# Attention weights divided by their row sum in front of the transposes, with scores and e in a tile per head

## The chip, the cores and the metric

The kernel runs on one core of one Trainium2 chip. The metric is the device time of one execution in microseconds (us); shorter is better. The kernel before takes 1104.95 us (median of three runs, 1103.55 to 1105.52).

## The reference

Thresholded attention with 4 batches, 8 heads, 576 positions and 64 channels per head, and behind it two feed-forward blocks on 2304 tokens:

```python
scale = 1.0 / np.sqrt(q.shape[-1])
scores = scale * np.matmul(q, k.transpose(0, 1, 3, 2))
thresh = np.max(scores, axis=-1, keepdims=True) - tau
scores = np.where(scores >= thresh, scores, -1000000000.0)
scores = scores - np.max(scores, axis=-1, keepdims=True)
attn = np.exp(scores)
attn = attn / (np.sum(attn, axis=-1, keepdims=True) + 1e-09)
x = np.matmul(attn, v)          # then x[tokens, heads * 64]
h = ((x @ w1) * (x @ w2)) @ w3 @ w_out
g = h @ w_in;  out = np.maximum(0.01 * g, g) @ w_out2
```

All inputs and the output are float32. Only the lines from `scores` to `x` are touched by the change.

## The kernel before

**Staging.** The program has two large stages. Up to about 640 us it runs the attention, and between the attention's instructions TensorE gets pieces of other work, called fillers: first the folding of w3 with w_out into one matrix (`fold_weights`, tiles ps34), then, for each batch and each of two groups of queries, the first feed-forward block (`gated`, tiles psab and psh). From about 700 us on it runs the second feed-forward block. Weights arrive as raw words and are decoded on ScalarE, VectorE and GpSimd (`stream`, L142 to L153), mostly in the first 130 us.

**Units and steps.** Heads are taken in pairs. The 576 queries of a pair are two groups: 256 queries (two chunks of 128) and 320 queries (two chunks of 128 and one of 64). A unit is one pair and one group, 32 units in all. A step is one chunk. In the 64 steps with a full chunk both heads are computed one beside the other. The 64-query chunk has one step for both heads (`c is None`): its two 64-row halves are laid over the 128 partitions through the tile qz, so it counts as one head. There are 16 such steps, 80 steps in all.

**One step.** `scores` computes the scores of a chunk of queries against all 576 keys into the PSUM tile sc (one bank per half of the keys and head), takes the negated maximum nm of each row (VectorE, L225), the threshold th (L226), and e = exp(score - max) (ScalarE, L227). `mask` sets e to zero below the threshold and adds up each row as it goes (VectorE, L241). `transposes` turns e by matmuls against an identity matrix into tp and tq, and copies these into HH and tl, with keys on the partitions. Once a unit's steps are done, `weighted` multiplies with v into the PSUM tile av, 128 channels of two heads by the unit's queries.

**The division.** It stands behind all this. av holds queries along the columns, while the row sums lie along the partitions. So `reciprocals` spreads 1 / sum on GpSimd over a tile rb, and `normalise`, a step after `weighted`, turns rb by matmuls (L322, L324) into the PSUM tile bc, multiplies xs, ScalarE's copy of av, with it on VectorE (L325), casts the product on ScalarE (L327) and has GpSimd subtract the cast from it (L328). Cast and rest are x, the input of `gated`.

**Buffers.** The pool ps_w has two PSUM buffers named w. They are shared by the fillers' sums (ps34, psab, psh), av and bc. The pool ps_a has one buffer each for sc, tp and tq. e has two buffers of two heads each.

**Order.** TensorE's instructions stand in the order in which the code is written; so do SP's until the loop has started the second `gated`. For the other engines a scheduler orders the instructions; each engine then runs its own in order. The loop of step n writes for TensorE: scores(n + 1), `weighted` of the unit that has ended, filler, first head's transposes of n, filler, second head's transposes, `normalise`, filler. So scores(n + 1) stand one step ahead of the transposes of n, and wait until mask(n) has read sc.

Of the kernel before, what the change touches and what calls it, by code (L numbers as in the profile page):

```python
# [8 lines left out]
F32 = mybir.dt.float32  # L9
# [30 lines left out]
def attention_gated_ffn(ctx: ExitStack, tc: tile.TileContext, qkv, tau, w3t, wout, w12, w2, out):  # L40
# [27 lines left out]
    pairs = cpool.tile([P, D], F32, name="pairs")
    nc.vector.tensor_tensor(out=pairs, in0=ident[:, :D], in1=ident[:, D:], op=ALU.add)
    sides = cpool.tile([P, P], F32, name="sides")  # L70
    nc.vector.memset(sides, 0.0)
    nc.vector.memset(sides[:D, :D], 1.0)
    nc.vector.memset(sides[D:, D:], 1.0)
# [4 lines left out]
    one = cpool.tile([P, 1], F32, name="one")  # L78
    nc.vector.memset(one, 1.0)
    tauc = cpool.tile([P, 1], F32, name="tauc")  # L80
    neg = cpool.tile([P, 1], F32, name="neg")
    scl = cpool.tile([P, 1], F32, name="scl")
# [116 lines left out]
            nc.vector.tensor_scalar(out=q, in0=q, scalar1=scl, scalar2=None, op0=ALU.mult))  # L199


    sc_t, e_t, stat = {}, {}, {}

    def scores(n):

        pair, g, c = STEPS[n]
        u = units.index((pair, g))
        qk = qk_t[u]
        heads = range(1 if c is None else 2)
        sc = ps_a.tile([P, 2, 2, 512], F32, tag="sc", name="sc")  # L210
        for half in range(2):
            ks = slice(half * HS, half * HS + HS)
            for a in heads:
                if c is None:
                    nc.tensor.matmul(sc[:, a, half, :HS], qz[u % 2], qk[:, ks], start=True, stop=True)
                else:
                    r = slice(a * D, a * D + D)
                    o = S + Q0[c] - GROUPS[g][0]
                    nc.tensor.matmul(sc[:, a, half, :HS], qk[r, o:o + P], qk[r, ks], start=True, stop=True)  # L219
        e = apool.tile([P, 2, S], F32, tag="e", name="e", bufs=2)  # L220
        ths = []
        for a in heads:
            nm = apool.tile([P, 1], F32, tag="nm", name="nm", bufs=4)
            th = apool.tile([P, 1], F32, tag="th", name="th", bufs=4)
            nc.vector.tensor_reduce(out=nm, in_=sc[:, a, :, :HS], op=ALU.max, axis=AX.XY, negate=True)  # L225
            nc.vector.tensor_scalar(out=th, in0=nm, scalar1=-1.0, scalar2=cb, op0=ALU.mult, op1=ALU.add)  # L226
            nc.scalar.activation(  # L227
                e[:, a].rearrange("p (a b) -> p a b", a=2), sc[:, a, :, :HS], AF.Exp, bias=nm)
            ths.append(th)
        sc_t[n], e_t[n] = (sc, ths), e  # L230

    def mask(n):
        pair, g, c = STEPS[n]
        sc, ths = sc_t.pop(n)
        key = (pair, g)
        if key not in stat:
            stat[key] = apool.tile([P, 5], F32, tag="stat", name="stat", bufs=4)
        for a, th in enumerate(ths):
            ev = e_t[n][:, a].rearrange("p (a b) -> p a b", a=2)
            o = 4 if c is None else 2 * (c % 2) + a  # L240
            nc.vector.scalar_tensor_tensor(  # L241
                out=ev, in0=sc[:, a, :, :HS], scalar=th, in1=ev, op0=ALU.is_ge, op1=ALU.mult,
                accum_out=stat[key][:, o:o + 1])

    he_t = {}

    def transposes(n):

        pair, g, c = STEPS[n]
        if (pair, g) not in he_t:
            he_t[pair, g] = apool.tile([P, 4, 2, 320], F32, tag="HH", name="HH")
        HH, tail = he_t[pair, g], tl[pair % 2]
        e = e_t.pop(n)
        tq = ps_a.tile([P, 2, P], F32, tag="tq", name="tq")
        if c is None:
            tp = ps_a.tile([P, 4, P], F32, tag="tp", name="tp")
            for kc in range(4):  # L260
                nc.tensor.transpose(tp[:, kc], e[:, 0, kc * P:kc * P + P], ident)
            nc.tensor.transpose(tq[:, 0], e[:, 0, S - P:], ident)
            nc.scalar.copy(HH[:, :, :, :D], tp.rearrange("p k (a w) -> p k a w", a=2))
            nc.vector.tensor_copy(
                tail[D:, :, :D], tq[D:, 0].rearrange("p (a w) -> p a w", a=2))
            yield
            return
        o = Q0[c] - GROUPS[g][0]
        for a in range(2):
            tp = ps_a.tile([P, 4, P], F32, tag="tp", name="tp")  # L270
            for kc in range(4):
                nc.tensor.transpose(tp[:, kc], e[:, a, kc * P:kc * P + P], ident)  # L272
# [4 lines left out]
            nc.tensor.transpose(tq[:, a], e[:, a, S - P:], ident)  # L277
            if a:
                nc.scalar.copy(tail[D:, :, o:o + P], tq[D:])
            yield  # L280

    xs_t, x_t, rb_t = {}, {}, {}

    def weighted(pair, g):

        gw = GROUPS[g][1]
        vv = vv_t[units.index((pair, g))]
        HH, tail = he_t.pop((pair, g)), tl[pair % 2]
        av = ps_w.tile([P, 512], F32, tag="w", name="av")
        for i in range(NK):  # L290
            for a in (1, 0):
                kc = (4, 0, 1, 2, 3)[i]
                rhs = (HH[:, kc, a] if kc < 4 else tail[:, a])[:, :gw]
                nc.tensor.matmul(  # L294
                    av[a * D:a * D + D, :gw], vv[:, a, kc], rhs, start=(i == 0), stop=(i == NK - 1))
        xs = apool.tile([P, 320], F32, tag="xs", name="xs", bufs=2)
        nc.scalar.copy(xs[:, :gw], av[:, :gw])
        xs_t[pair, g] = xs

    def reciprocals(pair, g):  # L300

        st = stat.pop((pair, g))
        n = 4 + g
        rr = apool.tile([P, 5], F32, tag="rr", name="rr", bufs=2)
        nc.vector.tensor_scalar(out=rr[:, :n], in0=st[:, :n], scalar1=1e-9, scalar2=None, op0=ALU.add)
        nc.vector.reciprocal(rr[:, :n], rr[:, :n])
        rb = apool.tile([P, 3, P], F32, tag="rb", name="rb")
        nc.gpsimd.tensor_tensor(
            out=rb[:, :2].rearrange("p c (h d) -> p (c h) d", h=2),
            in0=rr[:, :4].unsqueeze(2).to_broadcast([P, 4, D]),  # L310
            in1=one.unsqueeze(2).to_broadcast([P, 4, D]), op=ALU.mult)
        if g:
            nc.gpsimd.tensor_tensor(
                out=rb[:, 2], in0=rr[:, 4:5].to_broadcast([P, P]), in1=sides, op=ALU.mult)
        rb_t[pair, g] = rb

    def normalise(pair, g):
        gq, gw, cs = GROUPS[g]
        xs, rb = xs_t.pop((pair, g)), rb_t.pop((pair, g))
        bc = ps_w.tile([P, 512], F32, tag="w", name="bc")  # L320
        if g:
            nc.tensor.matmul(bc[:, :D], rb[:, 2], pairs, start=True, stop=True)  # L322
        for i, c in enumerate(cs):
            nc.tensor.transpose(bc[:, Q0[c] - gq:Q0[c] - gq + P], rb[:, i], ident)  # L324
        nc.vector.tensor_tensor(out=xs[:, :gw], in0=xs[:, :gw], in1=bc[:, :gw], op=ALU.mult)  # L325
# [130 lines left out]
    keep_busy(9)  # L456
    scores(0)
    keep_busy(10)
    weigh, norm = [], []
    filler = iter(())  # L460
    queue = []
    rate, due = 0.0, 0.0
    for n in range(NS):
# [27 lines left out]
        fill(1)  # L491
        for _ in pieces:
            pass
        if norm:
            normalise(*norm.pop())
        if last_of_unit:
            reciprocals(pair, g)
            weigh.append((pair, g))
        elif u and STEPS[n - 1][:2] != (pair, g):
            norm.append(units[u - 1])  # L500
        fill(2)
        if n < 3:
            keep_busy(7)
# [165 lines left out]
```

## Time and profile before

| | |
|---|---|
| median of three runs | 1104.95 us |
| the profiled execution | 1104.54 us |
| its span | 1102.7 us |
| TensorE matmuls busy | 1065.0 us, 97% |
| VectorE busy | 508.8 us, 46% |
| ScalarE busy | 474.0 us, 43% |
| GpSimd busy | 256.8 us, 23% |
| chain that ended last: share of TensorE | 81% |

The profile names the engines PE (TensorE's matmuls), PEld (its weight loads, which run beside the matmuls), DVE (VectorE), ACT (ScalarE), POOL (GpSimd) and SP. Times are from the start of the span. A row names the line, the engine, the operation, the tile written and the tiles read; `[1.75 <-DVE e L241]` says that the engine was idle for 1.75 us before and what it waited for. PEclk is the granted share of TensorE's clock. Matmuls overlap and their ends are modelled, so distances between starts say more than their lengths.

### The profile page before, as it was taken

To read this page: it belongs to the slowest core of one execution; us is meant where nothing else is said; L and a number is where in the kernel's file an instruction comes from. 1 tells how busy PE (TensorE), PEld (TensorE's weight loads), DVE (VectorE), ACT (ScalarE), POOL (GpSimd) and SP (SyncE) were. 2 spreads that over 40 slices of the span, in tenths; PEclk is the share of its full clock that TensorE was granted. 3 is DMA by queue.
4 is the path that set the end of the run, shared out by engine and by line. 5 is a ranking of instruction groups with operands and counts; after the bars stand their busy time and mean duration, and the time that the engine had idled before them with its cause. 6 is when DMAs were issued, how large, how long until landed. Compare 5 with 4: busy or idle time off the path is not lost.

```text
span 1102.7 us, 16185 instructions
## 1 busy us (share of the span) xinstructions
PE 1065.0 (97%) x6368; PEld 864.2 (78%) x6368; DVE 508.8 (46%) x1087; ACT 474.0 (43%) x891; POOL 256.8 (23%) x256
## 2 busy tenths in 40 slices
PE   7999799999998999999999999999999999999998
PEld 5555487789877888877898789877888888888887
DVE  5767766554666555664556633365311211111111
ACT  4767744343444444443444443477422222222232
POOL 2536712021211120120212146477400100000000
PEclk7999899999999999998999999999999999999999
DMA  9654610312112212111120023356200110010010
GB/s 305 199 198 130 204 54 23 81 35 65 40 40 63 59 30 65 44 54 51 38 62 25 1 79 114 102 191 201 72 13 1 34 34 1 5 44 1 1 39 20
DMA packets 35099, 77.59 MB, mean 70 GB/s; under 512 B 4560, under 2 KB 19408, under 8 KB 32976
## 3 DMA queue, kind: packets, MB, share of 16 engines
q1 hardware_dynamic: 34880, 76.56, 22.0%
q8 instruction: 50, 0.82, 0.3%
q14 instruction: 25, 0.20, 0.1%
q10 hardware_dynamic: 144, 0.00, 0.0%
HBM read 67.11 MB, written 9.44 MB: 69 GB/s over the span
## 4 chain that ended last, share of the span: by engine, by line
PE 81%; DVE 7%; ACT 6%; DMA 2%; issue 2%; POOL 1%; ACTq 0%; SPq 0%; DVEq 0%; POOLq 0%
PE psab L383 16%; PE po L606 16%; PE ps L584 16%; PE psh L402 9%; PE av L294 7%; PE sc L219 7%; PE tp L272 4%; PE ps L361 4%; DVE e L241 2%; ACT e L227 1%; DVE t L145 1%; ACT t L142 1%; PE tq L277 1%; ACT lw L144 1%; ACT HH L276 1%
## 5 line engine op out<-in xcount | busy, mean ns | idle before, releaser
L383 PE MATMUL psab<-x,w 128*128 128x256 f32 (+1 forms) x1536 | 234.5, 303 | 2.9 <-DVE xs L325 2.0
L383 PEld LDWEIGHTS psab<-x,w 128*128 128x128 f32 x1536 | 208.9, 189 | 24.9 <-issue 15.9
L584 PE MATMUL ps<-h,w 128*128 128x512 f32 (+1 forms) x960 | 215.7, 370 | 0.4 <-POOL w L153 0.3
L606 PE MATMUL po<-w,gg 128*128 128x512 f32 x864 | 213.8, 392 | 1.8 <-ACT gg L591 1.8
L584 PEld LDWEIGHTS ps<-h,w 128*128 128x128 f32 x960 | 169.0, 188 | 36.3 <-POOL w L153 1.3
L606 PEld LDWEIGHTS po<-w,gg 128*128 128x128 f32 x864 | 159.2, 188 | 38.1 <-ACT gg L591 3.3
L592 DVE TENSOR_TENSOR gg<-gf,gg 128x512 fp32r<-128x512 f32 (+1 forms) x80 | 61.2, 765 | 270.0 <-ACT gg L591 268.4
L225 DVE TENSOR_REDUCE nm<-sc 128x1 f32<-128x576 f32 x144 | 108.8, 756 | 108.3 <-PE sc L219 66.7
L227 ACT ACTIVATE e<-sc,nm 128x576 f32<-128x576 f32 x144 | 107.0, 743 | 117.3 <-DVE nm L225 117.0
L589 ACT ACTIVATE gf<-ps 128x512 f32<-128x512 f32 (+1 forms) x80 | 44.2, 554 | 227.0 <-PE ps L584 227.0
L241 DVE SCALAR_TENSOR_TENSOR e<-sc,th,e 128x576 f32<-128x576 f32 x144 | 112.7, 815 | 46.5 <-ACT e L227 46.5
L402 PE MATMUL psh<-gt,w 128*128 128x256 f32 (+1 forms) x768 | 115.1, 301 | 0.6 <-ACT ht L409 0.5
L394 POOL TENSOR_TENSOR gt<-at,gt 128x256 fp32r<-128x256 f32 (+1 forms) x64 | 52.7, 824 | 264.3 <-ACT gt L393 264.3
L402 PEld LDWEIGHTS psh<-gt,w 128*128 128x128 f32 x768 | 104.1, 189 | 7.7 <-issue 5.4
L219 PE MATMUL sc<-qk 64*128 64x288 f32 x512 | 81.7, 438 | 15.1 <-DVE e L241 11.2
L272 PE MATMUL tp<-ident,e 128*128 128x128 f32 x512 | 79.1, 278 | 6.0 <-ACT HH L276 6.0
L272 PEld LDWEIGHTS tp<-ident,e 128*128 128x128 f32 x512 | 61.9, 143 | 16.2 <-ACT HH L276 8.5
L151 POOL TENSOR_TENSOR lw<-t,lw 128x512 int32<-128x512 int32 x48 | 66.0, 1380 | 25.6 <-ACT lw L144 15.2
L219 PEld LDWEIGHTS sc<-qk 64*128 64x128 f32 x512 | 44.9, 188 | 33.9 <-issue 9.5
L294 PE MATMUL av<-HH,vv 128*64 128x256 f32 (+1 forms) x512 | 69.8, 416 | 0.0
L561 POOL TENSOR_TENSOR h<-hr,h 128x1024 fp32r<-128x1024 f32 (+1 forms) x10 | 23.8, 2380 | 188.2 <-DVE h L560 188.2
L361 PE MATMUL ps<-wo,w 128*128 128x512 f32 x128 | 60.0, 614 | 5.3 <-DVE xs L325 4.7
(72 smaller groups left out, 989.0 us busy)
## 6 DMA issues: line engine op xcount, KB each, us to landing
st<-in_w SPq DMA_DIRECT2D x40, 512.0 KB, 4.6
vv<-in_qkv SPq DMA_DIRECT2D x64, 160.0 KB, 2.4
raw<-in_w3t SPq DMA_DIRECT2D x8, 1024.0 KB, 5.8
qk<-in_qkv SPq DMA_DIRECT2D x32, 208.0 KB, 3.5
qk<-in_qkv SPq DMA_DIRECT2D x32, 144.0 KB, 3.0
out<-os SPq DMA_DIRECT2D x18, 256.0 KB, 2.1
raw<-in_wout SPq DMA_DIRECT2D x4, 1024.0 KB, 11.3
raw<-in_w SPq DMA_DIRECT2D x4, 1024.0 KB, 6.2
```

The costliest lines, as they stand in the source:

```text
L151: nc.gpsimd.tensor_tensor(out=lw, in0=t, in1=lw, op=ALU.add)
L219: nc.tensor.matmul(sc[:, a, half, :HS], qk[r, o:o + P], qk[r, ks], start=True, stop=True)
L225: nc.vector.tensor_reduce(out=nm, in_=sc[:, a, :, :HS], op=ALU.max, axis=AX.XY, negate=True)
L227: nc.scalar.activation(e[:, a].rearrange("p (a b) -> p a b", a=2), sc[:, a, :, :HS], AF.Exp, bias=nm)
L241: nc.vector.scalar_tensor_tensor(out=ev, in0=sc[:, a, :, :HS], scalar=th, in1=ev, op0=ALU.is_ge, op1=ALU.mult, accum_out=stat[key][:, o:o ...
L272: nc.tensor.transpose(tp[:, kc], e[:, a, kc * P:kc * P + P], ident)
L294: nc.tensor.matmul(av[a * D:a * D + D, :gw], vv[:, a, kc], rhs, start=(i == 0), stop=(i == NK - 1))
L361: nc.tensor.matmul(ps, w3_t[i][:, j * P:j * P + P], wo_t[j // 2][:, (j % 2) * 512:(j % 2) * 512 + 512], start=(j == 0), stop=(j == KF - 1))
L383: nc.tensor.matmul(ps[:, :gw], w12_t[i][:, a, mat * 512 + kk * P:mat * 512 + kk * P + P], xt[kk][:, c, :gw], start=(m == 0), stop=(m == 11))
L402: nc.tensor.matmul(ps[:, :gw], w34_t[i // 2][:, a, i % 2, o * P:o * P + P], gt[i][:, c, :gw], start=(m == 0), stop=(m == 23))
L584: nc.tensor.matmul(ps[:, :tw], w2_t[j][:, a, kk * P:kk * P + P], h3_t[ci][:, c, kk, :tw], start=(m == 0), stop=(m == 11))
L606: nc.tensor.matmul(po_t[t], gg[:, c, t * P:t * P + P], w2_t[j][:, a, 512:], start=(j == 0 and (a, c) == PASSES[0]), stop=(j == KF2 - 1 and ...
```

## The change

The row sum that `mask` accumulates goes into a small tile rr of two columns, one per head. A new function `even_out` adds 1e-9, takes the reciprocal, and multiplies e by it, per partition: the first head on VectorE, the second on ScalarE. It is written behind scores(n + 1), ahead of the transposes of n. sc and e become one tile per head (tags sc0, sc1, e0, e1; the space is the same). `reciprocals`, `normalise`, their tiles and constants go. `weighted` now casts av to x on ScalarE, straight from PSUM, and VectorE subtracts the cast from av.

```diff
-        sc = ps_a.tile([P, 2, 2, 512], F32, tag="sc", name="sc")
+        sc = [ps_a.tile([P, 2, 512], F32, tag=f"sc{a}", name="sc") for a in heads]
...
-        e = apool.tile([P, 2, S], F32, tag="e", name="e", bufs=2)
+        e = [apool.tile([P, S], F32, tag=f"e{a}", name="e", bufs=2) for a in heads]
...
+        rr = rr_t[n] = apool.tile([P, 2], F32, tag="rr", name="rr", bufs=2)
         for a, th in enumerate(ths):
...
-                out=ev, in0=sc[:, a, :, :HS], scalar=th, in1=ev, op0=ALU.is_ge, op1=ALU.mult,
-                accum_out=stat[key][:, o:o + 1])
+                out=ev, in0=sc[a][:, :, :HS], scalar=th, in1=ev, op0=ALU.is_ge, op1=ALU.mult,
+                accum_out=rr[:, a:a + 1])
+
+    def even_out(n):
+        rr, heads = rr_t.pop(n), 1 if STEPS[n][2] is None else 2
+        nc.vector.tensor_scalar(
+            out=rr[:, :heads], in0=rr[:, :heads], scalar1=1e-9, scalar2=None, op0=ALU.add)
+        nc.vector.reciprocal(rr[:, :heads], rr[:, :heads])
+        nc.vector.tensor_scalar(
+            out=e_t[n][0], in0=e_t[n][0], scalar1=rr[:, :1], scalar2=None, op0=ALU.mult)
+        if heads > 1:
+            nc.scalar.activation(e_t[n][1], e_t[n][1], AF.Copy, scale=rr[:, 1:2])
...
-        xs = apool.tile([P, 320], F32, tag="xs", name="xs", bufs=2)
-        nc.scalar.copy(xs[:, :gw], av[:, :gw])
-        xs_t[pair, g] = xs
-
-    def reciprocals(pair, g):
...
-    def normalise(pair, g):
...
         x = xpool.tile([P, 2, 320], F32R, tag="x", name="x")
-        nc.scalar.copy(x[:, 0, :gw], xs[:, :gw])
-        nc.gpsimd.tensor_tensor(
-            out=x[:, 1, :gw], in0=xs[:, :gw], in1=f(x[:, 0, :gw]), op=ALU.subtract)
+        nc.scalar.copy(x[:, 0, :gw], av[:, :gw])
+        nc.vector.tensor_tensor(
+            out=x[:, 1, :gw], in0=av[:, :gw], in1=f(x[:, 0, :gw]), op=ALU.subtract)
...
         if n + 1 < NS:
             scores(n + 1)
+        even_out(n)
...
-        if norm:
-            normalise(*norm.pop())
         if last_of_unit:
-            reciprocals(pair, g)
             weigh.append((pair, g))
-        elif u and STEPS[n - 1][:2] != (pair, g):
-            norm.append(units[u - 1])
```

**How the order of the instructions moves.** TensorE, the last step of a unit of the first group and the single-head scores behind it, in the kernel before (sc is written from qz, psab are filler sums):

```order
L383 MATMUL psab<-x,w_855 128x256 x12
L272 MATMUL tp<-ident,e 128x128 x4
L277 MATMUL tq<-ident,e 128x128
L322 MATMUL bc<-pairs,rb 128x64
L324 MATMUL bc<-ident,rb 128x128 x2
L383 MATMUL psab<-x,w_855 128x256 x12
L215 MATMUL sc<-qk,qz_93 128x288 x2
L383 MATMUL psab<-x,w_874 128x256 x12
```

The same place now:

```order
L354 MATMUL psab<-x,w_861 128x256 x12
L273 MATMUL tp<-ident,e 128x128 x4
L278 MATMUL tq<-ident,e 128x128
L354 MATMUL psab<-x,w_861 128x256 x12
L207 MATMUL sc<-qk,qz_87 128x288 x2
L354 MATMUL psab<-x,w_880 128x256 x12
```

The two rows of bc are gone; nothing else on TensorE has changed its place.

VectorE, in the last step of a later unit of the first group, in the kernel before (L241 is the mask, L194 and L199 scale the queries of the next unit, L391 is the product of `gated`):

```order
L225 TENSOR_REDUCE nm<-sc 128x1
L226 TENSOR_SCALAR th<-nm,cb 128x1
L225 TENSOR_REDUCE nm<-sc 128x1
L226 TENSOR_SCALAR th<-nm,cb 128x1
L241 SCALAR_TENSOR_TENSOR e,stat<-sc,th,e 128x576 x2
L194 TENSOR_SCALAR qz_93<-qk,scl 64x64 x2
L199 TENSOR_SCALAR qk<-qk,scl 128x256
L305 TENSOR_SCALAR rr<-stat 128x4
L306 RECIPROCAL rr<-rr 128x4
L391 TENSOR_TENSOR at<-psab,at 128x320
L274 COPY HH<-tp 128x4x128
```

Now (L217 is the maximum, L229 the mask, L238 to L241 are `even_out`, L299 is the subtraction of x, L362 the product of `gated`):

```order
L217 TENSOR_REDUCE nm<-sc 128x1 x2
L218 TENSOR_SCALAR th<-nm,cb 128x1 x2
L229 SCALAR_TENSOR_TENSOR e,rr<-sc,th,e 128x576 x2
L186 TENSOR_SCALAR qz_87<-qk,scl 64x64 x2
L191 TENSOR_SCALAR qk<-qk,scl 128x256
L238 TENSOR_SCALAR rr<-rr 128x2
L299 TENSOR_TENSOR x<-av,x 128x256
L240 RECIPROCAL rr<-rr 128x2
L241 TENSOR_SCALAR e<-e,rr 128x576
L362 TENSOR_TENSOR at<-psab,at 128x320
L275 COPY HH<-tp 128x4x128
```

Both maxima now stand ahead of both thresholds; the reciprocal stands behind the subtraction of x, and the scaling of e ahead of the product of `gated` and of the copy into HH.

## Rows read from the trace of the kernel before

**Rows 1.** Busy us (x instructions) by engine: PE, PEld, DVE, ACT, POOL; clock; DMA.

```profile
110.00:130.00 20.00, 13.11 (x45) 7.18 (x44) 15.38 (x27) 15.55 (x29) 17.23 (x15) 0.83 0.66 196
130.00:640.00 510.00, 496.96 (x3665) 417.15 (x3663) 307.37 (x754) 223.92 (x441) 90.20 (x127) 0.99 0.16 48
```

**Rows 2.** PE's waits to 700 us: line, releaser, total us, times, longest.

```profile
PE sc L219 <- DVE e L241: 11.2, 8, 2.5
PE tp L272 <- ACT HH L276: 6.0, 7, 2.2
PE ps L361 <- DVE xs L325: 4.7, 1, 4.7
...
PE psab L383 <- DVE xs L325: 2.0, 8, 0.3
```

**Rows 3.** Timeline of weight loads, 408 to 424 us: start, us, instruction, [idle before].

```profile
410.06 0.25 PEld L324 LDWEIGHTS bc<-ident,rb 128*128 128x128 f32 x2
410.28 1.77 PEld L402 LDWEIGHTS psh<-gt,w 128*128 128x128 f32 x12
...
422.88 0.50 PEld L272 LDWEIGHTS tp<-ident,e 128*128 128x128 f32 x4
```

**Rows 4.** Timeline of weight loads, 144 to 149 us.

```profile
144.69 0.30 PEld L322 LDWEIGHTS bc<-pairs,rb 128*128 128x128 f32 x2
...
145.08 1.49 PEld L383 LDWEIGHTS psab<-x,w 128*128 128x128 f32 x12
146.55 0.78 PEld L215 LDWEIGHTS sc<-qk,qz 128*128 128x128 f32 x4
148.03 1.12 PEld L383 LDWEIGHTS psab<-x,w 128*128 128x128 f32 x9 [0.70 <-DVE xs L325]
```

**Rows 5.** Timeline of weight loads, 429 to 431 us.

```profile
429.52 0.82 PEld L215 LDWEIGHTS sc<-qk,qz 128*128 128x128 f32 x4
430.39 0.79 PEld L383 LDWEIGHTS psab<-x,w 128*128 128x128 f32 x5
```

**Rows 6.** Timeline of VectorE, 413 to 419 us: one step's two heads.

```profile
415.10 0.76 DVE L225 TENSOR_REDUCE nm<-sc 128x1 f32<-128x576 f32 x1 [0.56 <-ACT e L227]
...
416.90 0.82 DVE L241 SCALAR_TENSOR_TENSOR e<-sc,th,e 128x576 f32<-128x576 f32 x1 [0.79 <-ACT e L227]
...
417.64 0.81 DVE L241 SCALAR_TENSOR_TENSOR e<-sc,th,e 128x576 f32<-128x576 f32 x1
```

**Rows 7.** Three stretches from a step's scores to the group behind av.

```profile
206.99:212.10 5.11, 5.11 (x28) 2.64 (x28) 2.41 (x6) 1.94 (x3) 0.86 (x1) 0.67 0.26 75
358.48:361.96 3.48, 3.48 (x29) 2.04 (x29) 1.94 (x4) 1.20 (x2) 0.86 (x1) 1.00 0.20 57
508.36:514.91 6.55, 6.55 (x29) 3.37 (x29) 3.36 (x8) 1.94 (x3) 0.86 (x1) 0.52 0.23 62
```

**Rows 8.** Timeline of PE, 112 to 127.3 us: the decode stage.

```profile
118.42 8.98 PE L361 MATMUL ps<-wo,w 128*128 128x512 f32 x16 [4.73 <-DVE xs L325]
```

**Rows 9.** Groups by line to 700 us: xcount | busy us, mean ns | idle before.

```profile
L241 DVE SCALAR_TENSOR_TENSOR e<-sc,th,e 128x576 f32<-128x576 f32 x144 | 112.7, 815 | 46.5 <-ACT e L227 46.5
...
L227 ACT ACTIVATE e<-sc,nm 128x576 f32<-128x576 f32 x144 | 107.0, 743 | 117.3 <-DVE nm L225 117.0
...
L226 DVE TENSOR_SCALAR th<-nm,cb 128x1 f32<-128x1 f32 x144 | 30.7, 213 | 4.2
...
L325 DVE TENSOR_TENSOR xs<-xs,bc 128x256 f32<-128x256 f32 (+1 forms) x32 | 14.3, 445 | 6.3 <-ACT ht L409 6.3
...
L327 ACT CAST x<-xs 128x256 fp32r<-128x256 f32 (+1 forms) x32 | 13.8, 432 | 44.1 <-DVE xs L325 43.8
...
L199 DVE TENSOR_SCALAR qk<-qk,scl 128x256 f32<-128x256 f32 x32 | 11.2, 352 | 1.9 <-DMA qk<-in_qkv 1.5
```

**Rows 10.** Timeline of VectorE, 113 to 117 us.

```profile
113.43 2.57 DVE L194 TENSOR_SCALAR qz<-qk,scl 64x64 f32<-64x64 f32 x2
```

**Rows 11.** Timeline of VectorE, 400 to 402 us.

```profile
400.77 0.53 DVE L194 TENSOR_SCALAR qz<-qk,scl 64x64 f32<-64x64 f32 x2
```

More of the change, by code (lines that the diff above doesn't have):

```diff
@@ L67, in attention_gated_ffn @@
     make_identity(nc, ident)
[L68 to L73, printed above, removed]
     qz = [cpool.tile([P, P], F32, name=f"qz{i}") for i in range(2)]
@@ L77, in attention_gated_ffn @@
         nc.vector.memset(t, 0.0)
-    one = cpool.tile([P, 1], F32, name="one")
-    nc.vector.memset(one, 1.0)
     tauc = cpool.tile([P, 1], F32, name="tauc")
@@ L214, in scores @@
                 if c is None:
-                    nc.tensor.matmul(sc[:, a, half, :HS], qz[u % 2], qk[:, ks], start=True, stop=True)
+                    nc.tensor.matmul(sc[a][:, half, :HS], qz[u % 2], qk[:, ks], start=True, stop=True)
                 else:
@@ L218, in scores @@
                     o = S + Q0[c] - GROUPS[g][0]
-                    nc.tensor.matmul(sc[:, a, half, :HS], qk[r, o:o + P], qk[r, ks], start=True, stop=True)
-        e = apool.tile([P, 2, S], F32, tag="e", name="e", bufs=2)
+                    nc.tensor.matmul(sc[a][:, half, :HS], qk[r, o:o + P], qk[r, ks], start=True, stop=True)
+        e = [apool.tile([P, S], F32, tag=f"e{a}", name="e", bufs=2) for a in heads]
         ths = []
@@ L224, in scores @@
             th = apool.tile([P, 1], F32, tag="th", name="th", bufs=4)
-            nc.vector.tensor_reduce(out=nm, in_=sc[:, a, :, :HS], op=ALU.max, axis=AX.XY, negate=True)
+            nc.vector.tensor_reduce(out=nm, in_=sc[a][:, :, :HS], op=ALU.max, axis=AX.XY, negate=True)
             nc.vector.tensor_scalar(out=th, in0=nm, scalar1=-1.0, scalar2=cb, op0=ALU.mult, op1=ALU.add)
             nc.scalar.activation(
-                e[:, a].rearrange("p (a b) -> p a b", a=2), sc[:, a, :, :HS], AF.Exp, bias=nm)
+                e[a].rearrange("p (a b) -> p a b", a=2), sc[a][:, :, :HS], AF.Exp, bias=nm)
             ths.append(th)
@@ L232, in mask @@
     def mask(n):
-        pair, g, c = STEPS[n]
         sc, ths = sc_t.pop(n)
-        key = (pair, g)
-        if key not in stat:
-            stat[key] = apool.tile([P, 5], F32, tag="stat", name="stat", bufs=4)
+        rr = rr_t[n] = apool.tile([P, 2], F32, tag="rr", name="rr", bufs=2)
         for a, th in enumerate(ths):
-            ev = e_t[n][:, a].rearrange("p (a b) -> p a b", a=2)
-            o = 4 if c is None else 2 * (c % 2) + a
+            ev = e_t[n][a].rearrange("p (a b) -> p a b", a=2)
             nc.vector.scalar_tensor_tensor(
-                out=ev, in0=sc[:, a, :, :HS], scalar=th, in1=ev, op0=ALU.is_ge, op1=ALU.mult,
-                accum_out=stat[key][:, o:o + 1])
+                out=ev, in0=sc[a][:, :, :HS], scalar=th, in1=ev, op0=ALU.is_ge, op1=ALU.mult,
+                accum_out=rr[:, a:a + 1])
+    rr_t = {}
+    def even_out(n):
[7 more added lines that the diff above has]
+            nc.scalar.activation(e_t[n][1], e_t[n][1], AF.Copy, scale=rr[:, 1:2])
     he_t = {}
@@ L260, in transposes @@
             for kc in range(4):
-                nc.tensor.transpose(tp[:, kc], e[:, 0, kc * P:kc * P + P], ident)
-            nc.tensor.transpose(tq[:, 0], e[:, 0, S - P:], ident)
+                nc.tensor.transpose(tp[:, kc], e[0][:, kc * P:kc * P + P], ident)
+            nc.tensor.transpose(tq[:, 0], e[0][:, S - P:], ident)
             nc.scalar.copy(HH[:, :, :, :D], tp.rearrange("p k (a w) -> p k a w", a=2))
@@ L271, in transposes @@
             for kc in range(4):
-                nc.tensor.transpose(tp[:, kc], e[:, a, kc * P:kc * P + P], ident)
+                nc.tensor.transpose(tp[:, kc], e[a][:, kc * P:kc * P + P], ident)
             if a:
@@ L276, in transposes @@
                 nc.scalar.copy(HH[:, :, a, o:o + P], tp)
-            nc.tensor.transpose(tq[:, a], e[:, a, S - P:], ident)
+            nc.tensor.transpose(tq[:, a], e[a][:, S - P:], ident)
             if a:
@@ L295, in weighted @@
                     av[a * D:a * D + D, :gw], vv[:, a, kc], rhs, start=(i == 0), stop=(i == NK - 1))
-        xs = apool.tile([P, 320], F32, tag="xs", name="xs", bufs=2)
-        nc.scalar.copy(xs[:, :gw], av[:, :gw])
-        xs_t[pair, g] = xs
-    def reciprocals(pair, g):
[L302 to L307, printed above, removed]
-        nc.gpsimd.tensor_tensor(
[L309 to L315, printed above, removed]
-    def normalise(pair, g):
[L318 to L325, printed above, removed]
         x = xpool.tile([P, 2, 320], F32R, tag="x", name="x")
-        nc.scalar.copy(x[:, 0, :gw], xs[:, :gw])
-        nc.gpsimd.tensor_tensor(
-            out=x[:, 1, :gw], in0=xs[:, :gw], in1=f(x[:, 0, :gw]), op=ALU.subtract)
+        nc.scalar.copy(x[:, 0, :gw], av[:, :gw])
+        nc.vector.tensor_tensor(
+            out=x[:, 1, :gw], in0=av[:, :gw], in1=f(x[:, 0, :gw]), op=ALU.subtract)
         x_t[pair, g] = x
@@ L458, in attention_gated_ffn @@
     keep_busy(10)
-    weigh, norm = [], []
+    weigh = []
     filler = iter(())
@@ L527, in attention_gated_ffn @@
     weighted(*weigh.pop())
-    run(filler, 2)
-    normalise(B * 4 - 1, 1)
     pe_order.close()
```

4 lines of the change are left out of this document (2 added, 2 removed).

## The prediction

> **What bounds the kernel now.** I read the busy time by stretch first. From 130 to 640 us, the steady part of the attention, TensorE is busy 496.96 of 510 us at a granted clock of 0.99, VectorE 307 and ScalarE 224 [rows 1]; from 110 to 130 us, while weights are still decoded, TensorE has 13.1 of 20 us, the clock is 0.83, and VectorE, ScalarE and GpSimd are each busy for over three quarters of the time [rows 1]. So TensorE is the bound, and the end moves by two things only: what is taken out of its queue, and what it waits for. Then I read its waits: 11.2 us before score matmuls, for the masked e (L241); 6.0 us before transposes, for the copy of the transposes before them (HH); 4.7 us once and 2.0 us in eight pieces for xs (L325) [rows 2]. Three of these four rows belong to what the change touches. Last come the stretches around these waits, and a row for the price of each kind of instruction. Nothing behind 700 us is touched. SP issues the same loads and stores in the same order and the change adds no DMA, so the queues move only with the engines.
>
> **The sum, against the profiled execution: 1104.54 us (span 1102.7 and 1.84 around it; the median of the three runs shown is 1104.95).**
>
> *Taken out of TensorE.* In a unit of the first query group the two bc transposes hold the weight port from 410.06 to 410.28 us, when the next matmul group begins: 0.22 [rows 3]. In a unit of the second group the product with pairs is added: 144.69 to 145.08, 0.39 [rows 4]. There are 16 units of each: 3.5 + 6.2 = 9.7 us. In some four places TensorE waits right behind bc anyway, so I count 8.3.
>
> *The buffer of bc.* After the single-head score matmuls the next group waits for xs, because bc sits in one of the two PSUM buffers w: 146.55 to 148.03, 1.48 us [rows 4]. Where nothing is awaited the same pair of starts is 429.52 to 430.39, 0.87 [rows 5]. Eight such waits [rows 2] times 0.61: 4.9. That buffer is then free; late next is its other user av, which VectorE's subtraction now releases instead of ScalarE's copy. Its next taker but one comes a filler group and the transposes later, more than 2 us, against 0.45 for the subtraction [rows 9] and what stands ahead of it. I count the 4.9 in full.
>
> *The scores' chain.* Today the second head's maximum waits 0.56 us for the first head's exp, and the first mask 0.79 for the second head's exp [rows 6], because both heads share a tile; the masks run from 416.90 to 418.45. With a tile per head the order on VectorE is maximum, maximum, th, th, mask, mask and the first mask needs only the first exp: the chain is 1.35 shorter. The score matmuls of the next step wait 11.2 us in 8 places for it [rows 2]. The longest, 2.5, is at the program's start; there the first transposes follow closely and will wait for the scaled e instead, so I count nothing. Of the other 8.7 in seven waits (1.24 on average, against 1.35) some are longer than average and keep a rest: 7.5 goes. Two of them are followed by a halved clock. The stretch of scores, av and the start of the next group takes 3.48 us at a clock of 1.00, but 5.11 at 0.67 and 6.55 at 0.52 [rows 7]; at 1.2 instead of 2.4 GHz for part of it, these two cost 4.7 more, of which I take 3.7 as regained. Together 11.2; the bounds are 0 and 13.4.
>
> *The decode stage.* At 118.42 TensorE has waited 4.73 us for xs behind decode work on VectorE [rows 8]. No bc, no such wait; but VectorE gets more work here, so I take 3.0, between 4.7 and a loss of 9 (below).
>
> *Added.* VectorE gets in each of 80 steps an addition and a reciprocal on two columns and a scaling of 128x576 in SBUF. The small ones cost what th costs, 0.21 each [rows 9]. The scaling has no row of its own: at least 0.35, the same operation on 256 columns (L199), at most 0.82, the mask on the same size with one more operand (L241) [rows 9]. From th to L199 the price rises by 0.14 for 255 columns, so 576 give an estimate of 0.53. That is 80 x 0.95 = 76 us, less the 32 pairs of the old reciprocals (about 13); the subtraction of x replaces the product with bc, 32 against 32, at 0.45 [rows 9]. From 130 to 640, where 68 of the steps and 27 of the pairs lie, VectorE goes from 307 to 307 + 65 - 11 = 361 us, 60 to 71%. ScalarE gets 64 scalings, between 0.43 (the cast of 256 or 320 columns, L327) and 0.74 (exp on 576) [rows 9]; I take 0.70, near the row of its size: 45 us, less 32 casts, about 31. GpSimd loses all its part in this. x is ready a step earlier than before, which nothing uses: the products that read it start two steps later as before. The cover is the distance from a step's last mask (418.45 [rows 6]) to its transposes (422.88 [rows 3]): 4.4 us for 0.95 of VectorE or 1.1 of ScalarE, filled by the next scores and a filler group. What stands behind the waiting scaling on ScalarE is the copies of at and HH, on VectorE the product for at, the copy HH and the next maxima. For the HH copies I let the 6.0 us [rows 2] double: +6.0. The bounds are 0 and 64 x 0.43 (below).
>
> Sum: 1104.5 - 8.3 - 4.9 - 11.2 - 3.0 + 6.0 = 1083.1. I forecast **1083 us**; with the bounds of the chain, the decode stage and the added waits this case reaches from 1073 to 1092.
>
> **Rivals.**
>
> *The waits come back behind the scaling.* TensorE loses its 8.3 us of work, but the scores and the buffers wait as before since VectorE is 11 points busier: only half of the 4.9 comes. 1104.5 - 8.3 - 2.5 = 1094. For it: VectorE's queue is in order. Against it: it idles 40% of that stretch.
>
> *GpSimd holds the scalings in the decode stage.* Two scalings of 64x64 take 2.57 us at 113.43 [rows 10] and 0.53 at 400.77 [rows 11], 1.0 more for each; in the first stretch GpSimd is busy 17.2 of 20 us [rows 1]. The new scaling is the same operation from SBUF. Thirteen steps lie before 130 us: 13 us if all of it lands on the path, and 1083 + 11 = 1094 if nearly all does. Against it: GpSimd has less to do there, and behind 130 us it is busy 90 of 510.
> The Trainium skill, GPSIMD Engine Reference, section 1 (Specifications), says that GpSimd shares its SBUF interfaces with VectorE and contends with VectorE instructions that read through two ports; by that rule, the trace agrees, every one of the 80 scalings is exposed, and the rule speaks against this change.
>
> *Transposes wait for the scaled e: slower.* In each of the 64 two-head steps the second head's transposes need mask, sum, reciprocal and ScalarE's scaling, which may stand behind copies. All gains together are 27.4 us, so it decides from 27.4 / 64 = 0.43 us a step; at 0.6 it gives 1104.5 - 27.4 + 38.4 = 1115.5. For it: a new wait in front of every transpose, on two queues. Against it: the 4.4 us of cover. Where fillers run out, av lies between instead.
>
> *The split does not free the heads:* maximum and exp still follow each other because both engines are taken up. Then the 11.2 stays: 1094.
>
> **Chances.** Forecast 0.55, waits come back 0.18, GpSimd 0.10, slower 0.12, no split 0.05. Change of less than 0.2%, about 2.2 us, is what a measurement of this kernel can't tell from none; of the second and third cases a small part falls there. Faster 0.82, same 0.06, slower 0.12. The range that leaves out 2 in 10 is 1072 to 1102.
>
> **What would show it.** Right: no bc on TensorE; the wait of the second maximum for exp gone; TensorE's waits for the mask under 4 us in all, most of it at the start; clock 1.00 where it was 0.67 and 0.52; the next group's start 0.87 us behind the single-head scores; the scaling at 0.5 to 0.6 us on VectorE and about 0.7 on ScalarE. Wrong: a row in TensorE's waits for the scaled e of more than 10 us; waits for HH or at well above 12; the first product of x later than 128 us, by which the decode stage would have lost; or a clock that falls in a new place.

## The result and the profile after

The changed kernel takes 1070.47 us (median of four runs, 1069.54 to 1072.44); beside it on the same chip the kernel before takes 1104.25 (1102.97 to 1105.52). The ratio is 0.9696, 95% interval 0.9678 to 0.9715: 33.8 us faster. The forecast was 21 us faster: the sign is right, and the time lies just below the range of 1073 to 1092. The profiled execution takes 1072.44 us with a span of 1070.6, 32.1 less than before.

Page of the changed kernel, part 1: busy us, share of the span, instructions of each engine.

```profile
PE 1047.0 (98%) x6272; PEld 852.5 (80%) x6272; DVE 556.8 (52%) x1258; ACT 506.4 (47%) x923; POOL 207.0 (19%) x176
```

VectorE and ScalarE do more (508.8 and 474.0 before). TensorE is busy 18 us less, which holds both what was taken out and what a higher clock shortens; the rest of the 32 us are 14 us of waits.

Changed kernel, busy time by stretch (PE, PEld, DVE, ACT, POOL; clock; DMA); the first two answer [rows 1], the other three are the stretches from scores to the group behind av of [rows 7].

```profile
110.00:130.00 20.00, 16.47 (x79) 10.66 (x79) 16.31 (x25) 16.56 (x31) 17.47 (x14) 0.91 0.75 218
130.00:640.00 510.00, 505.85 (x3748) 430.06 (x3745) 357.90 (x914) 263.04 (x490) 64.77 (x70) 1.00 0.19 56
...
195.55:199.03 3.48, 3.48 (x29) 2.04 (x28) 3.32 (x7) 2.45 (x4) 0.00 (x0) 1.00 0.27 77
339.17:342.64 3.47, 3.47 (x29) 2.03 (x28) 3.31 (x7) 2.44 (x4) 0.00 (x0) 1.00 0.20 55
482.78:486.26 3.48, 3.48 (x29) 2.04 (x28) 3.32 (x7) 2.45 (x4) 0.00 (x0) 1.00 0.21 56
```

From 130 to 640 us TensorE is idle for 4 us where it was idle for 13. The three stretches all take 3.48 us at a clock of 1.00, where they took 5.11, 3.48 and 6.55. VectorE has 358 us of 510 where 361 was forecast.

Changed kernel, TensorE's waits to 700 us (total, times, longest), as [rows 2].

```profile
PE tp L273 <- ACT HH L277: 8.2, 7, 2.2
PE psab L354 <- DVE w L338: 3.5, 1, 3.5
PE tp L273 <- DVE e L241: 2.2, 1, 2.2
...
PE sc L211 <- DVE e L229: 0.3, 1, 0.3
```

The 11.2 us for the masks are 0.3 now, the eight pieces for xs are gone, and the new wait that one rival feared, transposes for the scaled e, comes once in the whole program. The 4.7 us for xs in the decode stage are gone too, but 3.5 us for w (L338) stand there instead, at 122.60 us. L338 is VectorE's subtraction at the end of a folding sum, and it too stands behind decode work.

Changed kernel, weight loads, 139 to 142 us (start, us, instruction): the place of [rows 4].

```profile
139.74 0.79 PEld L207 LDWEIGHTS sc<-qk,qz 128*128 128x128 f32 x4
140.59 1.63 PEld L354 LDWEIGHTS psab<-x,w 128*128 128x128 f32 x12
142.16 0.46 PEld L273 LDWEIGHTS tp<-ident,e 128*128 128x128 f32 x4
```

0.85 us from the single-head scores to the next group, as forecast (0.87 in [rows 5], 1.48 in [rows 4]).

VectorE in the changed kernel: a scaling at the program's start; one beside the place above; and a step's two heads, as [rows 6].

```profile
13.02 1.45 DVE L241 TENSOR_SCALAR e<-e,rr 128x576 f32<-128x576 f32 x1
...
140.66 0.52 DVE L241 TENSOR_SCALAR e<-e,rr 128x576 f32<-128x576 f32 x1
...
393.37 1.42 DVE L217 TENSOR_REDUCE nm<-sc 128x1 f32<-128x576 f32 x2 [2.34 <-PE sc L211]
394.71 0.33 DVE L218 TENSOR_SCALAR th<-nm,cb 128x1 f32<-128x1 f32 x2
395.02 0.82 DVE L229 SCALAR_TENSOR_TENSOR e<-sc,th,e 128x576 f32<-128x576 f32 x1
```

The same step's first maximum in the kernel before:

```profile
413.54 0.76 DVE L225 TENSOR_REDUCE nm<-sc 128x1 f32<-128x576 f32 x1 [2.25 <-PE sc L219]
```

From the first maximum to the first mask it is 1.65 us now, 3.36 before (413.54 to 416.90). Both maxima follow each other without the 0.56, and the first mask follows without the 0.79.

Changed kernel, groups by line to 700 us (xcount | busy us, mean ns | idle before), as [rows 9].

```profile
L244 ACT ACTIVATE e<-e,rr 128x576 f32<-128x576 f32 x64 | 49.7, 776 | 54.5 <-DVE rr L240 54.5
L241 DVE TENSOR_SCALAR e<-e,rr 128x576 f32<-128x576 f32 x80 | 46.9, 586 | 2.5
...
L299 DVE TENSOR_TENSOR x<-av,x 128x256 fp32r<-128x256 f32 (+1 forms) x32 | 14.4, 451 | 5.6 <-ACT x L298 5.6
```

The scaling costs 0.52 on VectorE behind 130 us (estimate 0.53) and 0.78 on ScalarE (0.70). The mean of 586 ns holds 12 scalings before 130 us, some of which are longer (last section).

**Where the 32 us came from.** The starts of av's weight loads mark the 32 units. The distance between two neighbouring units is the time of one unit. Where the clock stays at 1.00 it repeats to 0.02 us from one batch to the next. Units count from 0. The columns between "before" and "changed" are runs that the next section describes: "scores alone" has only the scores' tile split, "a tile per head" has scores and e split, "division on e, shared tiles" has the moved division without any split. The two runs with "no division" leave it out.

| us from av to av | before | scores alone | a tile per head | division on e, shared tiles | no division, shared tiles | changed | changed, no division |
|---|---|---|---|---|---|---|---|
| 9 to 10, first group | 18.07 | 18.08 | 18.07 | 17.77 | 17.77 | 17.78 | 17.78 |
| 12 to 13, second group | 18.85 | 18.24 | 18.24 | 19.02 | 18.31 | 17.84 | 17.84 |
| 14 to 15, its last unit | 19.55 | 18.64 | 18.64 | 19.21 | 19.19 | 18.24 | 18.24 |
| 15 to 16, the next group's first | 16.48 | 14.95 | 14.95 | 16.48 | 17.54 | 14.61 | 14.55 |
| 16 to 17, the one behind it | 18.08 | 18.08 | 18.06 | 19.46 | 19.67 | 17.78 | 17.77 |
| start to unit 3 | 91.74 | 85.16 | 86.60 | 91.89 | 89.55 | 88.35 | 84.75 |
| unit 3 to 4, decode stage | 41.74 | 42.39 | 42.47 | 42.68 | 42.64 | 39.14 | 40.59 |
| unit 4 to 31 | 510.36 | 491.90 | 491.83 | 506.44 | 503.64 | 483.46 | 482.56 |

At unit 31 the changed kernel is 32.9 us ahead (643.84 against 610.95), and 0.8 of it is lost behind 611 us. In the two columns with shared tiles the unit 16 to 17 runs at a mean clock of 0.91 and 0.90, and the 17.54 at 0.92. The columns are read in what follows.

### The profile page after: what moved, and what is told of

Read it like the earlier page. It is cut to its first block, busy times and chain, and to the rows that moved or that the text cites. A ratio compares the mean times of both kernels' runs of the same rounds, so it can differ in the third digit from the quotient of the medians.

```text
span 1070.6 us, 16230 instructions
## 1 busy us (share of the span) xinstructions
PE 1047.0 (98%) x6272; PEld 852.5 (80%) x6272; DVE 556.8 (52%) x1258; ACT 506.4 (47%) x923; POOL 207.0 (19%) x176
## 4 chain that ended last, share of the span: by engine, by line
PE 86%; DVE 4%; ACT 4%; DMA 2%; issue 2%; POOL 1%; SPq 0%; ACTq 0%; DVEq 0%; POOLq 0%
PE psab L354 19%; PE po L571 16%; PE ps L549 16%; PE psh L373 9%; PE av L295 7%; PE sc L211 7%; PE tp L273 5%; PE ps L332 3%; PE sc L207 1%; DVE t L137 1%; PE tq L278 1%; DVE w L145 1%; ACT t L134 1%; DMA st<-in_w 1%; DMA raw<-in_wout 1%
## 5 line engine op out<-in xcount | busy, mean ns | idle before, releaser
L219 ACT ACTIVATE e<-sc,nm 128x576 f32<-128x576 f32 x144 | 103.4, 742 | 92.1 <-DVE nm L217 91.8
L217 DVE TENSOR_REDUCE nm<-sc 128x1 f32<-128x576 f32 x144 | 103.4, 753 | 80.5 <-PE sc L211 61.6
L229 DVE SCALAR_TENSOR_TENSOR e<-sc,th,e 128x576 f32<-128x576 f32 x144 | 114.5, 815 | 10.1 <-ACT e L219 9.9
L273 PEld LDWEIGHTS tp<-ident,e 128*128 128x128 f32 x512 | 61.6, 142 | 20.3 <-ACT HH L277 10.7
L244 ACT ACTIVATE e<-e,rr 128x576 f32<-128x576 f32 x64 | 49.7, 776 | 54.5 <-DVE rr L240 54.5
L295 PE MATMUL av<-HH,vv 128*64 128x256 f32 (+1 forms) x512 | 67.6, 406 | 0.0
## 6 DMA issues: line engine op xcount, KB each, us to landing
raw<-in_wout SPq DMA_DIRECT2D x4, 1024.0 KB, 10.7
```

The costliest lines, as they stand in the source:

```text
L217: nc.vector.tensor_reduce(out=nm, in_=sc[a][:, :, :HS], op=ALU.max, axis=AX.XY, negate=True)
L219: nc.scalar.activation(e[a].rearrange("p (a b) -> p a b", a=2), sc[a][:, :, :HS], AF.Exp, bias=nm)
L229: nc.vector.scalar_tensor_tensor(out=ev, in0=sc[a][:, :, :HS], scalar=th, in1=ev, op0=ALU.is_ge, op1=ALU.mult, accum_out=rr[:, a:a + 1])
L273: nc.tensor.transpose(tp[:, kc], e[a][:, kc * P:kc * P + P], ident)
L295: nc.tensor.matmul(av[a * D:a * D + D, :gw], vv[:, a, kc], rhs, start=(i == 0), stop=(i == NK - 1))
```

## The experiments

Ratios are against runs of the kernel before on the same chip, with 95% intervals. Four runs were made on one chip (both splits, the moved division alone, no division with the split, every scaling twice) and the other seven on another.

**The two halves of the change alone.** First the split without the moved division:

```diff
-        sc = ps_a.tile([P, 2, 2, 512], F32, tag="sc", name="sc")
+        sc = [ps_a.tile([P, 2, 512], F32, tag=f"sc{a}", name="sc") for a in heads]
-        e = apool.tile([P, 2, S], F32, tag="e", name="e", bufs=2)
+        e = [apool.tile([P, S], F32, tag=f"e{a}", name="e", bufs=2) for a in heads]
```

> The kernel before with scores and e in a tile per head; the division stays behind the product with v, through bc. Theory A (the split pays on its own: seven waits of the scores for the masks, 8.7, the two clock dips behind them, 4.7, and some 3 at the start, where the first av comes earlier): 1104 - 16 = about 1088, between 1085 and 1091; score matmuls wait under 1 us for masks up to 700 us. Rival B (the gain is the removal of bc, the split frees nothing because maximum and exp follow each other anyway): 1101 to 1105. Theory A': the start belongs to the removed division's setup and not to the split: 1091 to 1093.

Measured: 1080.9 us, 0.9807 (0.9787 to 0.9828): 21 us, more than expected. Then the moved division with both heads in one tile, as before:

```diff
-        sc = [ps_a.tile([P, 2, 512], F32, tag=f"sc{a}", name="sc") for a in heads]
+        sc = ps_a.tile([P, 2, 2, 512], F32, tag="sc", name="sc")
-        e = [apool.tile([P, S], F32, tag=f"e{a}", name="e", bufs=2) for a in heads]
+        e = apool.tile([P, 2, S], F32, tag="e", name="e", bufs=2)
```

> The changed kernel with scores and e of both heads in one tile each, as before; the division is still made on e in front of the transposes. Theory A: bc off TensorE 8.3, its buffer 4.9 and the wait of the decode stage 3, in all 16, are kept, the mask waits and clock dips return: 1104 - 16 = about 1088, from 1086 to 1092. As one tile holds both heads, the second head's scaling and the transposes of the first are tied to each other: if that shows, waits for e in front of transposes come up, each up to 0.8 us in 64 steps, and the time is 1100 or more. Rival B: 1071 to 1078.

Measured: 1103.59 us, 1.0016 (1.0003 to 1.0029). None of the 16 us that this half should have kept came. So the change is not the sum of its halves: 21 faster, 2 slower, together 33 faster.

The second group's units tell why. There the forecast had put 0.39 on bc and 0.61 on bc's buffer, both of them the moved division's. In the table the 0.61 goes with the split (18.85 to 18.24) while bc and its buffer are still there, and 0.40 more goes with bc (17.84). The rows of VectorE show what the buffer had waited for. Kernel before, VectorE, the place of [rows 4]:

```profile
146.53 0.69 DVE L274 COPY HH<-tp 128x512 f32<-128x512 f32 x1
147.23 0.35 DVE L199 TENSOR_SCALAR qk<-qk,scl 128x256 f32<-128x256 f32 x1
147.50 0.48 DVE L325 TENSOR_TENSOR xs<-xs,bc 128x320 f32<-128x320 f32 x1
```

With the scores' tile alone split, VectorE, the same place of a later unit of the second group:

```profile
284.87 0.68 DVE L274 COPY HH<-tp 128x512 f32<-128x512 f32 x1
285.46 0.18 DVE L306 RECIPROCAL rr<-rr 128x5 f32<-128x5 f32 x1
285.56 0.45 DVE L325 TENSOR_TENSOR xs<-xs,bc 128x320 f32<-128x320 f32 x1
```

Its weight loads there:

```profile
285.75 0.79 PEld L215 LDWEIGHTS sc<-qk,qz 128*128 128x128 f32 x4
286.60 0.55 PEld L383 LDWEIGHTS psab<-x,w 128*128 128x128 f32 x3
```

The product with bc starts 0.95 us behind the single-head scores before (147.50 against 146.55), and 0.19 ahead of them with the split. The wait for the buffer was VectorE's lateness from the two heads' chain, one more face of the shared tile. In the run with the moved division alone, bc is gone and that lateness shows elsewhere. Its waits of TensorE, 130 to 700 us:

```profile
PE sc L211 <- DVE e L229: 9.7, 7, 2.1
PE tp L273 <- DVE th L218: 4.0, 8, 0.5
...
PE sc L207 <- DVE qz L186: 1.5, 8, 0.3
```

Its VectorE at such a place (142 to 152 us):

```profile
148.81 0.74 DVE L217 TENSOR_REDUCE nm<-sc 128x1 f32<-128x576 f32 x1
149.46 0.93 DVE L241 TENSOR_SCALAR e<-e,rr 128x576 f32<-128x576 f32 x1
150.31 0.20 DVE L218 TENSOR_SCALAR th<-nm,cb 128x1 f32<-128x1 f32 x1
```

GpSimd there:

```profile
149.34 0.74 POOL L365 TENSOR_TENSOR gt<-at,gt 128x256 fp32r<-128x256 f32 x1 [3.89 <-ACT gt L364]
```

Its weight loads there:

```profile
150.51 0.42 PEld L273 LDWEIGHTS tp<-ident,e 128*128 128x128 f32 x4 [0.67 <-PE psab L354]
```

The scaling ends at 150.39 and the transposes start at 150.51; the row names th because th ended last, but the transposes read e. Eight places lose 0.5 us here and 0.2 for qz, where the changed kernel scales at 140.66 for transposes at 142.16. At all eight the late scaling also falls beside a GpSimd subtraction and takes 0.93 us instead of 0.52, which is 0.41 against the 0.5 lost. Scores wait for masks as before (9.7 us), and in the first unit of a group the mean clock falls to 0.91 (16 to 17: 19.46 us against 17.78).

**Which tile ties the heads.** In the kernel before, only one of the two tiles is split: first the scores' tile (the first line pair of the split's diff), then e (the second).

> The kernel before with a tile per head for the scores alone; e stays shared. Theory (each shared tile ties the heads at its own place: sc the second maximum to the first exp, 0.56 us a step; e the first mask to the second exp, 0.79): about 0.4 of the 21 us that both splits gave, 1091 to 1096, and the first mask still waits for the second exp. Rival (one of the two ties everything, and it is sc, because VectorE's order changes with it): 1080 to 1085.

> The kernel before with a tile per head for e alone; the scores stay shared. Theory of two ties: about 0.6 of the 21 us, 1086 to 1092; the second maximum still waits for the first exp, the first mask no longer for the second. Rival (sc ties everything): 1099 to 1103. Third possibility (e ties everything): 1080 to 1085.

Measured: scores alone 1080.14 us, 0.9786 (0.9771 to 0.9801); e alone 1102.26 us, 0.9987 (0.9976 to 0.9998). The scores' tile gives all of it, and the theory of two ties falls. With e split, VectorE still shows both waits, the second of them a mask that shares nothing but sc with the second exp:

```profile
414.23 0.76 DVE L225 TENSOR_REDUCE nm<-sc 128x1 f32<-128x576 f32 x1 [0.56 <-ACT e L227]
...
416.02 0.82 DVE L241 SCALAR_TENSOR_TENSOR e<-sc,th,e 128x576 f32<-128x576 f32 x1 [0.78 <-ACT e L227]
```

Both engines only read sc there, and the program lets readers of one PSUM tile on different engines take turns. The Trainium skill, PSUM — Partial Sum Buffer, section "PSUM bank collisions raise a hardware error", says that two engines may not touch one PSUM bank in the same partitions at the same time, reads included, so that such instructions must be ordered. It speaks of banks, and the two heads' scores lie in different banks: that rule does not ask for this order, and the runs with the split do without it.

**What the scaling costs.** The division is left out altogether (no bc either, so no row is divided by its sum), once with shared tiles, once with the split:

```diff
             scores(n + 1)
-        even_out(n)
```

> Tiles of scores and e shared by the heads as before, no bc, and the division left out altogether. Theory (with shared tiles the scaling on VectorE comes on top of a chain that is already late, and that gives the 12 us of bc back): without it 1086 to 1092, and the waits of the transposes for th (4.0) and of the single-head scores for qz (1.5) that the scaling had brought are gone. Rival (bc was worth nothing as long as the masks are late, scaling or not): 1099 to 1104.

> The changed kernel without even_out: the division by the sum is left out. It prices the added work. If the prediction's term for added waits (+6.0) was real and something else gave more: 1064 to 1066. If the added work is hidden but for the start (transposes waiting for the scaled e, 2.2, and stretched scalings beside GpSimd): 1067 to 1069. If it is hidden altogether: 1070 to 1071.

Measured: with shared tiles 1094.86 us, 0.9922 (0.9907 to 0.9937); with the split 1068.78 us, 0.9698 (0.9677 to 0.9719). In shared tiles the scaling costs 1.0016 - 0.9922, about 10 us by ratios of two chips, and eats what bc's removal gives (8.6). The traces show 5.2 us of it at unit 31 (641.01 against 635.83), but the profiled execution without division is the slowest of its six. The time lies between what theory and rival expected. On top of the split the moved division gives 12 us (21 to 33). What the 8.6 leave of these stays lost in shared tiles without the scaling too, since the masks are late either way (10.2 us in this run). Of the two waits that were to go with the scaling, the one of the transposes for th went, and the one of the single-head scores for qz (1.5) stayed. With the split, scaling or not is the same within the intervals. The changed kernel ran once more on the other chip, beside the runs with one split and with shared tiles:

> The changed kernel once more, beside the others on one chip, so that small differences can be read. Expected 0.968 to 0.971 of the kernel before. Against the kernel without the division (0.9698 of before): if the added work costs 3 us, as the first unit's start in the trace says, the ratio here is 0.972 to 0.973; if it costs nothing, 0.969 to 0.970.

Measured: 1070.31 us, 0.9696 (0.9680 to 0.9711). By the ratios, from two chips, the cost of the scaling is 0, give or take 3 us; the medians are 1.5 us apart, and 1068.78 lies where the division was expected to be hidden but for the start. What the traces show of it lies at the start: the first av is at 23.87 us without division and at 27.18 and 26.28 in two executions with it, unit 4 at 125.34 against 127.49 and 126.10. From unit 4 to 31 it is 482.56 against 483.46 and 482.76. TensorE's waits for HH are as long without the division, and longer with the scores' tile alone split, which has no scaling either. No division first, then scores alone:

```profile
PE tp L273 <- ACT HH L277: 8.4, 8, 2.3
...
PE tp L272 <- ACT HH L276: 10.7, 8, 2.4
```

**How much cover there is.** Every scaling is done twice, then four times; the added ones multiply by one:

```diff
+            nc.scalar.activation(e_t[n][1], e_t[n][1], AF.Copy, scale=rr1[:, :1])
+        nc.vector.tensor_scalar(
+            out=e_t[n][0], in0=e_t[n][0], scalar1=rr1[:, :1], scalar2=None, op0=ALU.mult)
```

> The changed kernel with every scaling done a second time by ones, on the same two engines: 0.52 more on VectorE in 80 steps, 0.78 more on ScalarE in 64. If the cover of 4.4 us between a step's last mask and its transposes holds: 1071 to 1075, some of it at the start. Rival (the transposes wait for the scaled e; the cover is used up by what stands in the queues): 64 x 0.5 to 0.8 on top, 1102 to 1122.

> The changed kernel with every scaling done four times (three of them by ones): 1.56 more on VectorE in 80 steps, 2.3 more on ScalarE in 64. Doubling cost 8 to 9 us, nearly all of it before 152 us. If the cover of 4.4 us between a step's last mask and its transposes is real, 1.1 + 2.3 = 3.4 on ScalarE still fits in most steps and VectorE (343 + 107 of 480 us in the steady stretch) still idles: 1095 to 1115, most of the loss again before 152 us. Rival (a scaling that is not hidden costs its whole length): 64 x 1.5 to 2.3 more than with doubled scalings: 1170 to 1220.

Measured: twice 1077.72 us, 0.9778 (0.9756 to 0.9800); four times 1116.73 us, 1.0130 (1.0110 to 1.0149). They lie 2.7 and 1.7 us above the ranges expected from the cover, and the rivals' are far off. Doubled, unit 5 to unit 31 takes 465.78 us against 464.91: 66 steps lose 0.9 in all. Nearly all of the 9 us is lost before 153 us, while weights are decoded: the unit 4 to 5 alone takes 23.63 us instead of 18.55, at a mean clock of 0.86. Four times, the same stretch takes 493.27: 28.4 us, or 0.43 a step for 1.56 more on VectorE and 2.3 on ScalarE. Its waits of TensorE, 152 to 700 us, show the cover used up:

```profile
PE tp L280 <- ACT HH L284: 10.9, 19, 1.1
PE tp L280 <- DVE e L250: 6.2, 8, 1.1
PE tp L280 <- DVE th L220: 4.2, 3, 1.4
```

**Two versions of the changed kernel.** In one, the first step's decode work goes behind its division, so that on VectorE and ScalarE the first scaling stands ahead of it. In the other, e goes back into one tile:

```diff
-        load_halves(kh // 2)
+        if n:
+            load_halves(kh // 2)
...
         even_out(n)
+        if n == 0:
+            load_halves(kh // 2)
```

> The changed kernel with the first step's decode work written behind its mask and division, so that on VectorE and ScalarE the first scalings no longer stand behind a decode that waits for its weights. If the 2 to 3 us by which the first product with v comes later than in the kernel without the division (26.3 to 27.2 against 23.9) are this wait: first product at 24 to 25, time 1067 to 1069, ratio 0.967 to 0.968. If the time is set further down, by the decode stage at 122 us: 0.969 to 0.970.

```diff
-        e = [apool.tile([P, S], F32, tag=f"e{a}", name="e", bufs=2) for a in heads]
+        e = apool.tile([P, 2, S], F32, tag="e", name="e", bufs=2)
```

> The changed kernel with e of both heads in one tile again; only the scores keep a tile per head. If the scores' tile alone tied the heads, as its run on the kernel before says: 0.969 to 0.971 of before, the same as the changed kernel. If a shared e ties the scaling of one head to the transposes of the other: waits for e in front of transposes, 0.975 or more.

Measured: 1070.24 us, 0.9711 (0.9693 to 0.9730), and 1071.27 us, 0.9717 (0.9696 to 0.9737). The first shows no gain: its wait for the scaled e is gone and its first av is at 25.59 us, not the 24 to 25 expected, while that place differs by 0.9 us between two executions of the changed kernel (26.28 and 27.18) and is at 28.41 with e shared. The second is not told apart from the changed kernel: no effect of e's tile shows here either. Nothing tried is faster than the changed kernel by more than the runs can tell.

## Why the prediction was right in sign and too small

The terms, against the landmarks of the table:

| term | forecast | measured | how |
|---|---|---|---|
| bc off TensorE | 8.3 | 8.9 | scores alone against changed: 8.4 from unit 4 to 31, 0.5 from unit 1 to 3 |
| bc's buffer | 4.9 | 4.7 | 0.59 in eight units, all with the split |
| masks and clock | 11.2 | 13.8 | before against scores alone from unit 4 to 31, 18.5, less the 4.7 |
| decode stage | 3.0 | 2.6 | unit 3 to 4; not apart from the start, below |
| start | 0 | 2.9 | 3.4 to unit 3, less bc's 0.5 |
| added waits | -6.0 | 0 | unit 4 to 31 is 0.2 to 0.9 shorter without division, which bc's row holds; the start's row holds the rest |

Measured is 32.9 in all, forecast 21.4: the forecast is 11.5 short.

- **"For the HH copies I let the 6.0 us double: +6.0" is the step that failed**, by 6 of the 11.5 us. HH's waits rose to 8.2, but they are 8.4 without any division and 10.7 with the scores' tile alone split: the scaling has no part in the rise. From unit 4 to 31 the scaling costs 0.2 to 0.9 us, and behind 153 us twice the scaling still fits. No row stood for the doubling, and the prediction's own cover, 4.4 us for 0.95 or 1.1, spoke against it. In shared tiles the scaling does cost, about 10 us, but not as waits for HH (9.4 with it, 8.7 without). The split makes the room in which the scaling hides.
- **The start, counted at nothing.** The 2.5 us of waiting for the mask went and a 2.2 for the scaled e came, as foreseen. But the split also ends the second maximum's wait for ScalarE, which at the start is busy decoding: there the tie cost more than in the steady part. In the kernel before, the second step's maximum waited 1.30 us instead of 0.56, and TensorE waited 3.9 us in all for queries (L199) that VectorE scales behind the masks. With the scores' tile split these 3.9 are 0.8, in the changed kernel 0.4. The split runs have their first av at 25.00 and 25.55 instead of 31.27, and with the scaling it is at 26.28 and 27.18. One sign of being wrong did come: the clock falls in a new place, to 0.91 in the unit 0 to 1 (1.00 before), and that unit takes 19.63 us instead of 18.48; in the second execution of the changed kernel it stays at 1.00, with 18.88. VectorE's second step and TensorE's waits in the kernel before:

```profile
16.14 0.76 DVE L225 TENSOR_REDUCE nm<-sc 128x1 f32<-128x576 f32 x1 [1.30 <-ACT e L227]
...
PE sc L219 <- DVE qk L199: 3.9, 3, 2.5
```

- **The decode stage**: the size came near, by another way. The wait for xs went, but 3.5 us for w (L338) came in its place, and 4.5 without any division, so it is not the scaling's. The run with the scores' tile alone split still waits 3.3 for xs and yet has unit 4 at 127.55, the changed kernel at 127.49. Start and decode stage together gave 6.0, and but for the 0.5 of unit 1 to 3 none of it is shown to be the removal of bc.
- **Masks and clock**: right mechanism, too small. The waits went almost to nothing and the clock is 1.00 at both places; "some keep a rest" was not so (0.3 us remain in all), and all of the clock's 4.7 us came back.
- **bc's buffer**: right size, wrong owner. It was counted as a gain of the removed bc. The split alone gives it. Without bc but with shared tiles, the unit 12 to 13 is 0.54 shorter even without division, and 0.40 of that is bc itself.
- **The scaling's prices** (0.53 and 0.70) measured 0.52 and 0.78, VectorE's load 358 against 361 us.
- **The rivals.** Waits that come back behind the scaling, and a slower kernel: both untrue of this change, but the first is what the moved division alone shows, at 1.0016. GpSimd does stretch scalings before 130 us (below), and the stretch up to unit 4 gained 6.0 all the same. That the split does not free the heads is refuted by the run of the split alone.

What stays open: whether the scaling costs nothing or up to 3 us, nearly all of it before unit 4, which the runs do not tell apart; and what the removal of bc is worth before unit 4.

## What to carry to other kernels

A wait that names a buffer is priced by asking what made its releaser late: here the buffer of bc, the masks and part of the start were one shared PSUM tile, which made a reader on one engine take turns with a reader on another. Where a change has a part that shortens an engine's chain and a part that adds work to that engine, the added work must be weighed against the cover of the shortened chain; the halves alone gave 21 and -2 us, both together 33. A small 2 by 2 of runs (each half alone, both, neither) shows such a thing at once. Where the clock stays the same, distances between repeated landmarks show it to 0.02 us, while totals vary by 2.

## What the runs showed of the hardware

The scaling at 13.02 us took 1.45 us, with GpSimd at work from 12.88 for 1.27; the one at 140.66 took 0.52 with GpSimd idle. In the changed kernel the 12 scalings before 130 us take 964 ns on average and the 68 behind it 520. Five of the 12 have no GpSimd instruction beside them and take 0.52 as well, so decoding alone does not stretch them. Six take 0.99 to 1.63: there a GpSimd instruction had begun already, or began within 0.04 us. That agrees with the contention named in the prediction (the Trainium skill, GPSIMD Engine Reference, section 1). Where it began 0.22 us or more behind the scaling (one of the 12, and three of the 68) the scaling took 0.51 to 0.52. The same shows in the run with the moved division alone, where eight late scalings take 0.93 us beside GpSimd. What the stretching alone costs the path was not measured; without the division altogether, unit 4 comes 0.8 to 2.2 us earlier.
